# A gated recurrence with a SoLU layer behind it: weight conversions in pairs, the second group's keys turned by VectorE, loads and products of ones rearranged

## The chip, the cores and the metric

The kernel runs on one core of a Trainium2 chip. The metric is the device time of one execution in microseconds (us). It is measured in several runs; the median counts. A profile is one further execution, recorded by the hardware profiler. Names of engines: PE or TensorE (matmuls), DVE or VectorE, ACT or ScalarE, POOL or GpSimd, SP or SyncE (it only issues transfers here).

## The reference

Two blocks, one behind the other. The first is a gated linear recurrence over 768 steps, for 4 batches and 8 heads of 48 channels. The second takes its result as 3072 tokens of 384 values, multiplies by `w_in` to 1024 values, weighs each by its softmax, normalises, scales by `g_ln` and multiplies by `w_out`.

```python
for t in range(S):
    state = alpha[:, :, t, :, None] * state + np.einsum('bhd,bhe->bhde', k[:, :, t], v[:, :, t])
    y[:, :, t] = np.einsum('bhd,bhde->bhe', q[:, :, t], state)
...
x = attn_out.transpose(0, 2, 1, 3).reshape(B * S, H * D)
h = x @ w_in
e = np.exp(h - np.max(h, axis=-1, keepdims=True))
solu = h * e / (np.sum(e, axis=-1, keepdims=True) + 1e-09)
mu, var = np.mean(solu, -1, keepdims=True), np.var(solu, -1, keepdims=True)
out = ((solu - mu) / np.sqrt(var + 1e-06) * g_ln) @ w_out
```

q, k, v and alpha are float32. `w_in` (384 x 1024), `w_out` (1024 x 384) and `g_ln` are of random numbers; the two matrices come as float64 and are made into float32 on the core.

## The kernel before

**Tiling.** The 768 steps are cut into 6 groups of 128. In each group the recurrence becomes matmuls: running products of alpha along time (`scan_back`, `scan_on`, line 204) scale queries and keys, `scores` multiplies them (L278), `masked` keeps the causal half (L289), `read_values` multiplies by the values (L333), and `read_state` adds what the state of the earlier groups gives (L333 too). `keys_back` turns the scaled keys for `next_state` (L371), which brings the state to the end of the group. A group's result x has 4 batches x 128 tokens. For it, 8 slices f of 128 of the 1024 values are made: `up_mm` (three matmuls of 128x512, L394), Exp on ACT (L408), the product h times e on VectorE (L409) and its square on ACT (L412). `down` multiplies a chunk of 128 tokens by `w_out` (L513), in two halves of four f. The sums over the 1024 values come from matmuls with ones (`array_sums` L439, `token_sums` L462).

**The order is written by hand.** Each engine runs its instructions in the order in which the program gives them, and a wait holds everything behind it on that engine. The transfers named below are all issued by SP, in program order too. The body of `fast_path` from L674 to L850 is group 0 and the way into group 1; behind L933 a plan of names runs for the rest. The change touches only the first part.

**Turning.** q, k and alpha come with time along the partitions and must lie with channels along them. Group 0 does this by TensorE (`turned`, L164: a matmul with the identity, 96 of them for one tensor), group 1's k and q too (L780, L793, L805); group 1's alpha and all of the later groups go through VectorE (`firsts` L179 and `lasts` L182, called by `alpha_T` and `keys_T`). `load_first` and `load` bring the two layouts that these need; `ends_of` is ACT's copy of the last 16 channels for `turned`. `apart` (L245) parts the last channels of two heads on ACT.

**Conversion of the weights.** `w_in` and `w_out` come in 8 pieces, 0 to 3 of `w_in` (two f each), 4 to 7 of `w_out` (two f each). `fetch(i, slot, n)` loads n pieces into slots of `room` (six of 1536 words). `bit(i, k)` is step k of 5 of piece i on VectorE: two steps make the upper word (L622, L626), one its exponent (L630), one adds the lower word scaled by it (L634), and the last the sum into place (L636). Each takes 768 elements a partition. Piece i works in the two `lots` of its parity. `in_range` checks the range on ACT (L604, L607). `scaled` multiplies `w_out` by `g_ln` on ACT (L643). `u_of` puts h times e into the slots of `room` that are free by then. In the loop L753 to L778 steps of the conversions stand behind each f, by the list at L758; before it, piece 0 runs at L739 and piece 1 at L744.

**Behind the loop** come the second half of the sums, `down` of the first chunks, `mean` (L657, L664: what the mean of the normalisation takes from the output, from all of `w_out`), and group 1's decay, keys and queries. Scaled queries leave by `move_lasts` (8 transfers, L232) and `move_firsts` (4, L237) into `q64`, and `decay` (L261, on POOL) needs the last of them; `read_state` needs both.

**warm** (L452) multiplies ones by ones while TensorE has nothing else, 14 times at the start and 4 times before the queries.

Of the kernel before, what the change touches and what calls it, by code (L numbers as in the profile page):

```python
# [9 lines left out]
FP = mybir.dt.float32  # L10
U8 = mybir.dt.uint8
U32 = mybir.dt.uint32
# [4 lines left out]
P = 128  # L17
# [15 lines left out]
def fast_path(ctx, tc, q, k, v, alpha, moe_w_in, moe_w_out, moe_g_ln, out):  # L33
# [414 lines left out]

    def warm(n, ps=ps_o, tag="o"):
        t = ps.tile([P, 512], FP, tag=tag, name="warm")  # L450
        for i in range(n):
            nc.tensor.matmul(t[:, 0:P], lhsT=ones, rhs=ones, start=True, stop=True)  # L452

    def token_sums(g):

# [117 lines left out]
    def fetch(i, slot, n=1):  # L573

        kind, f = pieces[i]
        w = n * F // (2 if kind else KC)
        raw = room[:, 1536 * slot : 1536 * (slot + n)].bitcast(U32).rearrange("p (c f w) -> p c f w", f=w, w=2)
        if kind:
            parts = [(slice(0, P), c, moe_w_out[(f + c) * P : (f + c + 1) * P, :]) for c in range(2)]
        else:  # L580
            parts = [(slice(0, P), c, moe_w_in[c * P : (c + 1) * P, f * P : f * P + w]) for c in range(KC)]
        for rows, c, src in parts:
            if float64:
                nc.sync.dma_start(out=raw[rows, c].rearrange("p f w -> p (f w)"), in_=src.bitcast(U32))
            else:
                dst = w_out[rows, f + c, 0:DM] if kind else w_in[rows, c, f * P : f * P + w]
                nc.sync.dma_start(out=dst, in_=src)
        for m in range(n):
            raws[i + m] = raw[:, :, w // n * m : w // n * (m + 1)]

    far = const.tile([P, len(pieces), 2], FP, name="far")
    made = {}
# [16 lines left out]
    def bits(i, steps=range(5)):  # L609
        for k in steps if float64 else ():  # L610
            bit(i, k)

    def bit(i, k):
        lo, hi = raws[i][:, :, :, 0], raws[i][:, :, :, 1]
        if k == 0:
            made[i] = [
                lots[2 * (i % 2) + x].rearrange("p (c f) -> p c f", c=hi.shape[1]) for x in range(2)
            ]
        top, low = made[i]
        bits_top = top.bitcast(U32)  # L620
        if k == 0:
            nc.vector.tensor_scalar(  # L622
                out=bits_top, in0=hi, scalar1=3, scalar2=0x3FFFFFF8, op0=ALU.logical_shift_left, op1=ALU.bitwise_and
            )
        elif k == 1:
            nc.vector.scalar_tensor_tensor(  # L626
                out=bits_top, in0=hi, scalar=0xC0000000, in1=bits_top, op0=ALU.bitwise_and, op1=ALU.bitwise_or
            )
        elif k == 2:
            nc.vector.tensor_scalar(  # L630
                out=low.bitcast(U32), in0=bits_top, scalar1=0xFF800000, scalar2=None, op0=ALU.bitwise_and
            )
        elif k == 3:
            nc.vector.scalar_tensor_tensor(out=low, in0=lo, scalar=2.0**-52, in1=low, op0=ALU.mult, op1=ALU.mult)  # L634
        else:
            nc.vector.tensor_tensor(out=place(i), in0=low, in1=top, op=ALU.add)  # L636

    def scaled(i):

# [10 lines left out]
    def mean(half):  # L650


        m = ps_h.tile([P, 512], FP, tag="h", name="sums")[:, 0:DM]
        if half == 0:
            for f in range(FC):
                r = quarter(f % 4)
                nc.tensor.matmul(  # L657
                    m[r], lhsT=ones[:, 0:32], rhs=w_out[:, f, 0:DM], start=f < 4, stop=f >= FC - 4,
                    tile_position=(0, r.start), skip_group_check=True,
                )  # L660
            made["m"] = work.tile([P, DM], FP, name="o_mean")
# [29 lines left out]
    nc.gpsimd.memset(kg, 0.0)  # L691
    load_v(0)
    fetch(0, 3)
    fetch(1, 4)
    fetch(2, 1, 2)
    nc.vector.memset(ones, 1.0)
    nc.vector.memset(small_ones, 1.0 / 32)
    nc.vector.memset(mhalf, -0.5)
    nc.vector.memset(w_out[:, :, DM : DM + 1], 1.0)

    def three(name, where):
        return [pool.tile([P, NP, P], FP, tag=tag, name=f"{name}{i}") for i, (pool, tag) in enumerate(where)]
# [20 lines left out]
    for i in (0, 2, 1):  # L723
        if i == 1:
            scan_on(0, i)
        part = slice(NP * i, NP * i + NP)
        nc.vector.tensor_tensor(
            out=qe[:, :, 0:P] if i == 2 else qv[:, part, 0:P], in0=t[i], in1=aT[:, part, 1:SW], op=ALU.mult
        )
        if i == 2:  # L730
            apart()
    scores(0, 0)
    t = [x.tile([P, NP, P], FP, tag=n, name="a_" + n) for x, n in ((ps_h, "h"), (ps_o, "o")) for _ in range(2)]
    scores(0, 1, t)
    read_begin()
    for half in range(2):
        masked(half, range(B - 1))
        masked_apart(half, B - 1)
    bits(0)  # L739
    read_values(0)  # L740
    gains()
    keys_back(0)
    in_range(0)
    bits(1)  # L744

    steps = [(i, step) for i in range(2, 8) for step in range(5)]
    checks = {0: [(2, 0)], 1: [(2, 1)], 2: [(3, 0)], 3: [(3, 1)], 4: [(1, 0), (1, 1)], 5: [(4, 0), (4, 1)]}

    def check(f):
        for i, part in checks.get(f, ()):  # L750
            in_range(i, (part,))

    for f in range(FC):  # L753
        up_mm(0, f)
        if f == 4:
            array_sums(0, 0)
        up_act(0, f, lambda: check(f))
        for _ in range((4, 2, 3, 3, 3, 3, 3, 9)[f]):  # L758
            step = steps.pop(0)
            if float64:  # L760
                bit(*step)
        if f == 0:
            next_state(0)
            fetch(4, 3)
            load_first(k, kn, 1)
            load_first(q, qn, 1)
            load(alpha, an, 1)
        elif f == 2:
            ends_k = ends_of(kn, "e")
        elif f == 3:  # L770
# [36 lines left out]
    hold(1)  # L807
    keys_back(1, three("tp", [(ps_a, "a2"), (ps_a, "a3"), (ps_h, "h")]))
    scan_on(1, 2)
    nc.vector.tensor_tensor(out=qe[:, :, 0:P], in0=tq[2], in1=aT[:, H:NB, 1:SW], op=ALU.mult)  # L810
# [656 lines left out]
```

## Time and profile before

| | |
|---|---|
| median of 3 runs | 366.96 us (366.78 to 367.19) |
| the profiled execution | 368.38 us |
| its span, first to last instruction | 366.6 us |
| granted TensorE clock | 0.998 |
| VectorE busy, 20 to 30 / 60 to 70 / 90 to 100 us | 9.58 / 9.79 / 9.83 of 10 |
| ACT busy, 40 to 50 / 50 to 60 us | 8.26 / 7.09 of 10 |
| first matmul with `w_in` | 29.64 us |
| last step of the conversions | ends at 63.92 us |
| `read_state` of group 1 | 88.63 us |
| first matmul of group 1 with `w_in` | 97.58 us |

A line of the timeline gives start and length in us, engine, line of the program and operation, the tile that is written and those that are read, the shape, and how many alike stand together (x). In brackets stands how long the engine had been idle before and what it waited for; "issue" means nothing that the profile shows. PE is the matmul, PEld the load of its weights. A float32 matmul makes two records, so x24 is twelve matmuls. The ends of matmuls are modelled, so the distance of two starts says more than a length. A DMA window lists what each queue moved in that stretch: packets, MB and the time of its packets as a share of 16 engines.

### The profile page before, as it was taken

How to read it: one execution, taken by the hardware profiler on the slowest of the kernel's cores; microseconds unless marked ns; L12 is line 12 of the kernel's file. 1: busy time of each engine (PE TensorE's matmuls, PEld its weight loads, DVE VectorE, ACT ScalarE, POOL GpSimd, SP SyncE). 2: the span in 40 equal slices, each digit the busy share in tenths (PEclk: the TensorE clock that was granted, in tenths of full speed). 3: DMA queues.
4: the chain of work that ended last, by engine and by line, in shares of the span. 5: the costliest groups of instructions: out<-in, count | busy, mean ns of one | idle time of the engine just before them, and what ended most of it. 6: DMA issues, size and time to landing. Idle time of an engine off the chain costs nothing. (4 is left out here: it accounts for less than half of the span.)

```text
span 366.6 us, 10041 instructions
## 1 busy us (share of the span) xinstructions
PE 358.0 (98%) x4341; PEld 216.0 (59%) x4341; DVE 243.9 (67%) x375; ACT 146.5 (40%) x262; POOL 130.3 (36%) x127
## 2 busy tenths in 40 slices
PE   8989999999999999999999999999999999999994
PEld 8866345666655566556475556575556565555552
DVE  0999989979997796936665946766946404445420
ACT  3637887372736261252531253531242222222110
POOL 7020000003368663764232763332773121233300
PEclk9999999999999999999999999999999999999999
DMA  9994997326196509354044454004042000000011
GB/s 178 186 333 139 194 302 156 88 59 146 68 222 133 131 4 192 90 123 123 5 108 92 103 115 113 21 25 88 21 96 66 0 25 1 23 21 22 23 46 51
DMA packets 72871, 36.06 MB, mean 98 GB/s; under 512 B 48232, under 2 KB 70000, under 8 KB 72816
## 3 DMA queue, kind: packets, MB, share of 16 engines
q1 hardware_dynamic: 71792, 34.39, 39.6%
q10 hardware_dynamic: 1024, 0.92, 0.8%
q8 instruction: 36, 0.59, 0.7%
q14 instruction: 19, 0.16, 0.1%
HBM read 25.30 MB, written 4.72 MB: 82 GB/s over the span
## 5 line engine op out<-in xcount | busy, mean ns | idle before, releaser
L513 PE MATMUL o<-w_out,room 128*128 128x385 f32 x384 | 133.8, 491 | 0.0
L394 PE MATMUL h<-x,w_in 128*128 128x512 f32 x288 | 131.6, 597 | 0.0
L513 PEld LDWEIGHTS o<-w_out,room 128*128 128x128 f32 x384 | 71.1, 189 | 55.2 <-issue 13.4
L394 PEld LDWEIGHTS h<-x,w_in 128*128 128x128 f32 x288 | 53.2, 189 | 58.0 <-issue 49.0
L409 DVE TENSOR_TENSOR room<-h,e 128x512 f32<-128x512 f32 x40 | 27.6, 690 | 72.7 <-ACT e L408 72.7
L408 ACT ACTIVATE e<-h 128x512 f32<-128x512 f32 x40 | 23.9, 598 | 98.9 <-PE h L394 98.9
L427 POOL TENSOR_TENSOR p<-p,e 128x512 f32<-128x512 f32 x30 | 43.1, 1437 | 20.3 <-ACT e L408 20.2
L412 ACT ACTIVATE u<-room 128x512 f32<-128x512 f32 x40 | 25.2, 630 | 37.0 <-DVE room L409 37.0
L552 POOL TENSOR_TENSOR r<-sums,mhalf 128x1 f32<-128x1 f32 x20 | 14.8, 740 | 67.9 <-DVE sums L543 67.7
L289 DVE TENSOR_TENSOR sT<-a,mask 128x512 f32<-128x512 f32 x43 | 26.7, 682 | 8.7 <-PE a L278 8.7
L204 DVE TENSOR_TENSOR_SCAN hT<-aT,unit 128x516 f32<-128x516 f32 x18 | 24.3, 1396 | 7.9 <-ACT aT L709 7.8
L204 DVE TENSOR_TENSOR_SCAN aT<-aT,seed 128x516 f32<-128x516 f32 x18 | 25.4, 1441 | 0.2
L225 POOL TENSOR_TENSOR kT<-kT,hT 128x1024 f32<-128x1024 f32 (+1 forms) x8 | 13.3, 1687 | 33.6 <-DVE kT L179 33.6
L278 PEld LDWEIGHTS a<-qv,kT 32*128 32x128 f32 x704 | 21.1, 186 | 6.8 <-issue 2.4
L427 DVE TENSOR_TENSOR p<-p,u 128x512 f32<-128x512 f32 x30 | 21.7, 723 | 5.1 <-ACT u L412 5.1
L333 PE MATMUL y<-sT,vn 128*32 128x128 f32 x768 | 23.3, 274 | 1.6 <-issue 1.4
L278 PE MATMUL a<-qv,kT 32*128 32x128 f32 x704 | 23.7, 279 | 0.2 <-ACT qv L245 0.2
L212 POOL COPY fend<-hT 128x12 f32<-128x12 f32 x6 | 3.0, 507 | 56.4 <-DVE hT L204 56.4
L333 PEld LDWEIGHTS y<-sT,vn 128*32 128x32 f32 x768 | 20.9, 110 | 3.5 <-issue 2.7
L196 ACT ACTIVATE sq<-an,mone 128x1536 uint8<-128x1536 f32 x12 | 18.9, 1572 | 0.2
L554 ACT ACTIVATE o_sb<-o,r 128x384 f32<-128x384 f32 x16 | 9.3, 580 | 18.5 <-POOL r L552 18.5
L261 POOL TENSOR_TENSOR state<-state,lot 128x384 f32<-128x384 f32 x10 | 8.8, 902 | 15.6 <-DMA lot<-qv 15.6
(150 smaller groups left out, 376.7 us busy)
## 6 DMA issues: line engine op xcount, KB each, us to landing
vn<-in_v_dram SPq DMA_DIRECT2D x24, 192.0 KB, 4.7
an<-in_alpha_dram SPq DMA_DIRECT2D x20, 192.0 KB, 4.0
out_dram<-o_sb SPq DMA_DIRECT2D x20, 192.0 KB, 1.9
room<-in_moe_w_out_dram SPq DMA_DIRECT2D x8, 384.0 KB, 5.6
kn<-in_k_dram SPq DMA_DIRECT2D x16, 192.0 KB, 4.8
qn<-in_q_dram SPq DMA_DIRECT2D x16, 192.0 KB, 3.8
lot<-qe SPq DMA_DIRECT2D x40, 64.5 KB, 2.1
lot<-qv SPq DMA_DIRECT2D x20, 129.0 KB, 2.4
```

The costliest lines, as they stand in the source:

```text
L196: nc.scalar.activation(out=sq, in_=x, func=AF.Relu, scale=sign, bias=mone, accum_out=over[:, g, i : i + 1])
L204: nc.vector.tensor_tensor_scan(out=o, data0=a, data1=s, initial=1.0, op0=ALU.mult, op1=ALU.add)
L278: nc.tensor.matmul(a[b][:, i], lhsT=kT[quarter(b), kb], rhs=qv[quarter(b), qb, 0:P], start=not last and not i, stop=bool(last), tile_posit ...
L289: nc.vector.tensor_tensor(out=sT[:, b, half * NP : half * NP + NP], in0=a[b], in1=mask[:, None, :].to_broadcast([P, NP, P]), op=ALU.mult,)
L333: nc.tensor.matmul(y_bank(b)[quarter(r), a], lhsT=lhsT, rhs=rhs, start=(b, r) not in begun, stop=stop, tile_position=(row, 32 * r), skip_g ...
L394: nc.tensor.matmul(h, lhsT=w_in[:, a, f * P : (f + 1) * P], rhs=d["x"][:, a].rearrange("p b t -> p (b t)"), start=(a == 0), stop=(a == KC ...
L408: nc.scalar.activation(out=e, in_=h, func=AF.Exp)
L409: nc.vector.tensor_tensor(out=u, in0=h, in1=e, op=ALU.mult)
L412: nc.scalar.activation(out=u2, in_=u, func=AF.Square)
L427: eng.tensor_tensor(out=p, in0=d[0][i] if f == 1 else p, in1=d[f][i], op=ALU.add)
L513: nc.tensor.matmul(d["o"][:, 0 : DM + 1], lhsT=u_of(g, f)[:, b * P : b * P + P], rhs=w_out[:, f], start=(f == 0), stop=(f == FC - 1), skip ...
L552: nc.gpsimd.tensor_tensor(out=r, in0=s[:, 3:4], in1=mhalf, op=ALU.pow)
```

## The change

- `warm` makes products up to 512 wide, four of the old ones in one.
- `fetch` lays several pieces one behind the other in `room`, each contiguous; before, the rows of two pieces lay side by side. So slot 1 and slot 2 each hold one piece.
- The loads of pieces 1, 2 and 3 are issued behind `apart` of group 0: ACT writes one column of slot 4 there, and the load into that slot waits for it.
- Piece 0 is converted in halves of 128 columns, in an order in which the first half ends two steps ahead of the second.
- Pieces 1 to 7 are converted with the steps of piece i + 1 between those of piece i; how many stand behind each f changes. Piece 7's last step goes to POOL.
- Checks and scalings on ACT move: piece 4 is checked at f 4, piece 1 at f 5, `scaled(4)` and `scaled(5)` come at f 6.
- `fetch` of piece 5 comes at f 1, alpha's load at f 3 behind piece 6. Group 1's k is loaded by `load` instead of `load_first`.
- `turned` of group 1's keys is left out; `keys_T(1)` stands behind the conversions.
- The order behind the loop: `down`, sums, two scalings, `down`, keys, sums by token, alpha, then all of q in one piece; the products of keys one step later than their scans; `scan_on(1, 0)` before the first product of queries. `mean` takes a bank of `ps_a`.

```diff
     def warm(n, ps=ps_o, tag="o"):
         t = ps.tile([P, 512], FP, tag=tag, name="warm")
-        for i in range(n):
-            nc.tensor.matmul(t[:, 0:P], lhsT=ones, rhs=ones, start=True, stop=True)
+        for c in range(0, n, 4):
+            w = P * min(4, n - c)
+            x = ones[:, None, :].to_broadcast([P, w // P, P])
+            nc.tensor.matmul(t[:, 0:w], lhsT=ones, rhs=x, start=True, stop=True)
...
-        raw = room[:, 1536 * slot : 1536 * (slot + n)].bitcast(U32).rearrange("p (c f w) -> p c f w", f=w, w=2)
+        raw = room[:, 1536 * slot : 1536 * (slot + n)].bitcast(U32)
+        raw = raw.rearrange("p (m c f w) -> p c m f w", m=n, f=w // n, w=2)
...
-            raws[i + m] = raw[:, :, w // n * m : w // n * (m + 1)]
+            raws[i + m] = raw[:, :, m]
...
-    def bit(i, k):
+    def bit(i, k, part=None):
...
+        if part is not None:
+            lo, hi, top, low, dst = (x[:, :, P * part : P * part + P] for x in (lo, hi, top, low, dst))
...
-            nc.vector.tensor_tensor(out=place(i), in0=low, in1=top, op=ALU.add)
+            (nc.gpsimd if i == 7 else nc.vector).tensor_tensor(out=dst, in0=low, in1=top, op=ALU.add)
...
-        m = ps_h.tile([P, 512], FP, tag="h", name="sums")[:, 0:DM]
+        m = ps_a.tile([P, 512], FP, tag="a3", name="sums")[:, 0:DM]
...
     fetch(0, 3)
-    fetch(1, 4)
-    fetch(2, 1, 2)
...
+    def fetch_more():
+        nc.scalar.copy(out=slots[4][:, 0:1], in_=parity[:, 0:1])
+        fetch(1, 4)
+        fetch(2, 1, 2)
...
             apart()
+            fetch_more()
...
-    bits(0)
+    bits((0, k, part) for k, part in ((0, 0), (0, 1), (1, 0), (1, 1), (2, 0), (2, 1), (3, 0), (4, 0), (3, 1), (4, 1)))
...
-    bits(1)
-
-    steps = [(i, step) for i in range(2, 8) for step in range(5)]
-    checks = {0: [(2, 0)], 1: [(2, 1)], 2: [(3, 0)], 3: [(3, 1)], 4: [(1, 0), (1, 1)], 5: [(4, 0), (4, 1)]}
+    steps = [(1, 0), (1, 1)]
+    for i in range(1, 8):
+        steps += [(i, 2), (i + 1, 0), (i, 3), (i + 1, 1), (i, 4)]
+    steps = [x for x in steps if x[0] < 8]
+    for a, b in (((2, 1), (1, 4)), ((6, 1), (5, 4))):
+        i, j = steps.index(a), steps.index(b)
+        steps[i], steps[j] = b, a
...
+    convert(5)
+    checks = {0: [(2, 0)], 1: [(2, 1)], 2: [(3, 0)], 3: [(3, 1)], 4: [(4, 0), (4, 1)], 5: [(1, 0), (1, 1)]}
 
     def check(f):
         for i, part in checks.get(f, ()):
             in_range(i, (part,))
+        if f == FC - 2:
+            scaled(4)
...
-        for _ in range((4, 2, 3, 3, 3, 3, 3, 9)[f]):
-            step = steps.pop(0)
-            if float64:
-                bit(*step)
+        convert((5, 2, 3, 3, 4, 3, 2, 8)[f])
         if f == 0:
             next_state(0)
             fetch(4, 3)
-            load_first(k, kn, 1)
+            load(k, kn, 1)
             load_first(q, qn, 1)
+        elif f == 1:
+            fetch(5, 1)
+        elif f == 3:
+            fetch(6, 2)
             load(alpha, an, 1)
-        elif f == 2:
-            ends_k = ends_of(kn, "e")
-        elif f == 3:
-            fetch(5, 1)
-            fetch(6, 2)
             ends_q = ends_of(qn, "u2")
         elif f == 5:
             fetch(7, 3)
             load_v(1)
         elif f == 6:
-            scaled(4)
-    tk = three("tp_k", [(ps_a, "a2"), (ps_a, "a3"), (ps_h, "h")])
-    turned(kn, ends_k, tk)
+            scaled(5)
+    down(0, 0)
+    array_sums(0, 1)
+    scaled(6)
+    scaled(7)
+    down(1, 0)
+    keys_T(1)
     load(k, kn, 2)
-    array_sums(0, 1)
-    scaled(5)
-    down(0, 0)
-    scaled(6)
+    token_sums(0)
     alpha_over(1)
-    token_sums(0)
     alpha_T(1)
     load(alpha, an, 2)
-    down(1, 0)
-    scaled(7)
-    tq = three("tp_q", [(ps_a, "a0"), (ps_a, "a1")])
-    turned(qn, ends_q, tq, range(H))
-    for i in range(3):
-        scan_back(1, i)
-        part = slice(NP * i, NP * i + NP)
-        nc.vector.tensor_tensor(out=kT[:, part], in0=tk[i], in1=hk[:, part], op=ALU.mult)
+    tq = three("tp_q", [(ps_a, "a0"), (ps_h, "h"), (ps_a, "a2")])
+    turned(qn, ends_q, tq)
+    for i in (0, 1, None, 2):
+        if i is not None:
+            scan_back(1, i)
+        for j in {1: (0,), None: (1,), 2: (2,)}.get(i, ()):
+            part = slice(NP * j, NP * j + NP)
+            nc.vector.tensor_tensor(out=kT[:, part], in0=kT[:, part], in1=hk[:, part], op=ALU.mult)
     inverses(1)
     mean(0)
...
-    tq += three("tp_q2", [(ps_h, "h")])
-    turned(qn, ends_q, tq, range(H, NB))
     down(1, 1)
     hold(1)
-    keys_back(1, three("tp", [(ps_a, "a2"), (ps_a, "a3"), (ps_h, "h")]))
+    keys_back(1, three("tp", [(ps_a, "a1"), (ps_a, "a3"), (ps_h, "h")]))
     scan_on(1, 2)
+    scan_on(1, 0)
...
     for i in range(2):
-        scan_on(1, i)
+        if i:
+            scan_on(1, i)
```

More of the change, by code (lines that the diff above doesn't have):

```diff
@@ L583, in fetch @@
             if float64:
-                nc.sync.dma_start(out=raw[rows, c].rearrange("p f w -> p (f w)"), in_=src.bitcast(U32))
+                nc.sync.dma_start(
+                    out=raw[rows, c].rearrange("p m f w -> p m (f w)"),
+                    in_=src.bitcast(U32).rearrange("p (m x) -> p m x", m=n),
+                )
             else:
@@ L607, in in_range, with bits @@
             nc.scalar.activation(out=sq, in_=sq, func=AF.Exp, scale=-(2.0**24), accum_out=far[:, i, 1:2])
-    def bits(i, steps=range(5)):
-        for k in steps if float64 else ():
-            bit(i, k)
-    def bit(i, k):
+    def bits(steps):
+        for x in steps if float64 else ():
+            bit(*x)
+    def bit(i, k, part=None):
         lo, hi = raws[i][:, :, :, 0], raws[i][:, :, :, 1]
-        if k == 0:
+        if k == 0 and not part:
             made[i] = [
@@ L618, in bit @@
             ]
+        dst = place(i)
         top, low = made[i]
+        if part is not None:
+            lo, hi, top, low, dst = (x[:, :, P * part : P * part + P] for x in (lo, hi, top, low, dst))
         bits_top = top.bitcast(U32)
@@ L743, in fast_path, with convert @@
     in_range(0)
-    bits(1)
-    steps = [(i, step) for i in range(2, 8) for step in range(5)]
-    checks = {0: [(2, 0)], 1: [(2, 1)], 2: [(3, 0)], 3: [(3, 1)], 4: [(1, 0), (1, 1)], 5: [(4, 0), (4, 1)]}
+    steps = [(1, 0), (1, 1)]
[5 more added lines that the diff above has]
+        steps[i], steps[j] = b, a
+    def convert(n):
+        bits(steps[:n])
+        del steps[:n]
+    convert(5)
+    checks = {0: [(2, 0)], 1: [(2, 1)], 2: [(3, 0)], 3: [(3, 1)], 4: [(4, 0), (4, 1)], 5: [(1, 0), (1, 1)]}
     def check(f):
```

## The prediction

> **What bounds the kernel now.** I read, in this order: busy time by engine; TensorE's timeline of the first 125 us (does it ever stop?); the timelines of VectorE and of the DMA queue in the same stretch; the DMA windows around the one stop.
>
> ```profile
> PE 358.0 (98%) x4341; PEld 216.0 (59%) x4341; DVE 243.9 (67%) x375; ACT 146.5 (40%) x262; POOL 130.3 (36%) x127
> 23.09 0.64 PE L333 MATMUL y<-sT,vn 128*32 128x128 f32 x14 [0.20 <-DVE sT L289]
> 25.15 3.04 PE L333 MATMUL y<-sT,vn 128*32 128x128 f32 x102 [1.41 <-issue]
> 29.64 2.74 PE L394 MATMUL h<-x,w_in 128*128 128x512 f32 x6
> ...
> 54.08 1.96 PE L164 MATMUL tp_k<-ident,kn 128*32 128x128 f32 x64
> 55.85 1.06 PE L164 MATMUL tp_k<-ident,e 128*32 128x128 f32 x32
> 56.73 1.90 PE L439 MATMUL quarters<-sT,ones 128*32 128x512 f32 x16
> ...
> 88.63 1.19 PE L333 MATMUL y<-lot,state 64*32 64x128 f32 x64
> ```
>
> After 25.15 no line has an idle note until the tail, so TensorE is the bound: every microsecond that it starts later, or that is taken from its list, counts, if its inputs keep up. The 1.41 us have no releaser. Around them the DMA window 22.0 to 22.7 shows one packet of the instruction queue among full data queues; the windows from 15 to 22 have none.
>
> ```profile
> q1 hardware_dynamic: 142, 0.26, 103.2%
> q8 instruction: 1, 0.02, 8.7%
> ```
>
> Next to TensorE stands VectorE, which has hardly a gap from 8.9 to 79 us. Its starts show two prices:
>
> ```profile
> 38.79 0.94 DVE L622 TENSOR_SCALAR lot<-room 128x768 uint32<-128x768 uint32 x1
> 57.33 0.56 DVE L630 TENSOR_SCALAR lot<-lot 128x768 uint32<-128x768 uint32 x1
> 57.92 0.96 DVE L634 SCALAR_TENSOR_TENSOR lot<-room,lot 128x768 f32<-128x768 uint32 x1
> 58.92 0.96 DVE L636 TENSOR_TENSOR w_out<-lot 128x768 f32<-128x768 f32 x1
> 59.80 0.55 DVE L622 TENSOR_SCALAR lot<-room 128x768 uint32<-128x768 uint32 x1
> ```
>
> L634 is followed by its reader L636 after 1.00 us; L636 by an unrelated instruction after 0.88. So a neighbour that reads the result costs 0.12 more. And L622 takes 0.94 for pieces 2 and 3, 0.56 for the others.
>
> Last, the chain that ends at read_state (88.63):
>
> ```profile
> 74.50 0.69 DVE L810 TENSOR_TENSOR qe<-tp_q,aT 128x512 f32<-128x512 f32 x1
> 75.26 5.26 SPq L232 DMA_DIRECT2D lot<-qe  x8
> 80.62 3.16 SPq L237 DMA_DIRECT2D lot<-qv  x4
> 85.18 1.65 POOL L261 TENSOR_TENSOR state<-state,lot 128x384 f32<-128x384 f32 x2 [12.38 <-DMA lot<-qv]
> ```
>
> qe ends at 75.19, the state is decayed at 86.83, and read_state could begin about 0.15 later: qe's end plus 11.8 = 87.0. TensorE came at 88.63, so 1.6 us of slack.
>
> **The Trainium skill.** "Runtime: NRT & Kernel Launch", Instruction fetch mechanics: instructions come in 16 KiB blocks of 256 over a DMA queue of the sequencer's own. The trace agrees (36 packets, 0.59 MB, 16 KB each); the page calls the cost mostly hidden, here it is 1.41 us. "VectorE: DVE Perf Modes", Mode 2×_2P: two read ports serve one tensor if the outermost dimension is even, or odd and equal in source and destination. Agrees: pieces 2 and 3 read 3 separate runs of 256 (odd) into one run of 768, 0.94 us; the single runs take 0.56. [...]
>
> **Part by part.**
>
> *Wide ones.* 14 and 4 products become 4 and 1; a product is two weight loads and two matmuls, so 13 fewer products are 52 fewer instructions. The columns stay, so the first warm keeps its 6.03 us (estimate): a shorter one gains nothing (alpha lands at 7.0, where ACT's copy waits 4.84 us for it), a longer one costs its excess. The second stands before a wait for qn.
>
> *w_in behind the parting.* One ACT copy of a column (about 0.2, in a gap of 0.93 before L297), then 6 of the 9 issues move from about 18 to 19.9. Nothing later on SP wants to go before 31. The packet at 22.68 came behind what was issued before its request, I take it: three or four w_in loads. Now only v and piece 0 are ahead, and the block boundary lies 52 instructions later. Bounds: stall 0 to 1.4; I take 0.2. Pieces 2 and 3 then land near 28, wanted from 30.4.
>
> *First half of piece 0.* Without the stop, batch 3's mask (POOL, done 24.42) is not late, and four batches of 16 products at 0.058 end at 26.5. Then tp_g 0.15 and keys_back 1.37 (28.27 to 29.64): h begins at 28.0, with the 0.2 at 28.2, so 1.44 earlier. Its weights: piece 0 in halves. 768 elements at 0.56/0.96 give 384 at about 0.36/0.56 (half of the slope); eight of ten steps from 24.15, with the 0.2 that L622 lost there to POOL (0.74 against 0.56), end at 27.6: in time. All ten take 4.4, against 4.25 before. If halves fell to the slower mode, 0.8 more, and h at 28.4.
>
> *Conversions side by side.* Pieces 1 to 7 had 28 dependent neighbours, 6 of them parted by L409; now 4 remain: 18 x 0.12 = 2.2. L622 of pieces 2 and 3: 2 x 0.38 = 0.76. Piece 7's addition goes to POOL: 0.88. The last conversion ended at 63.84: 63.84 - 3.84 = 60.0. VectorE's waits in this stretch were 1.37 (0.28, 0.16, 0.20, 0.36, 0.37). Walking the new order with h groups of 2.62 from 28.2, I find 0.1 at f 5, 0.6 at f 6 and 0.85 at f 7, because ACT has 3.2 to 3.4 us in each of f 4 to 6 against TensorE's 2.62 (four checks, then two scalings of 1.05, the second before the last Exp). So 1.5 against 1.4: no change, 60.0 stands.
>
> *Loads.* On SP k goes with the plain load (4 issues, 3.3 us), then q (4.4), piece 5, piece 6, then alpha (3.4), wanted at 61 only. Piece 5 is issued near 40 instead of 44 and wanted at 44.8; landing took 5.6: covered, barely. The moved in_range(1) frees slot 4 for u 6 in time.
>
> *Keys by VectorE.* TensorE loses 96 products, all that runs from 54.08 to 56.73: 2.65 us. VectorE gains two transposes, by the starts of the next group's (95.87, 97.76, 98.69) 2.82. The copy of k's ends leaves ACT (0.61). No matmul waits for them before keys_back. The products with hk then read kT from SBUF instead of PSUM: 0.69 as now, since L427's additions of that size from SBUF take 0.66 to 0.69. mean's bank moves to a3, free since the first group's a3 was read.
>
> *Order of the tail.* VectorE from 60.0: keys 2.82, cols 0.37, alpha 2.91, scans and products 1.15 + 1.15 + 0.61 + 0.61 + 1.27 + 0.61, reciprocal 0.26, two scans 2.30, qe 0.69: 74.75, against 75.19. qv's first part follows at 75.4, so scores are free. POOL's addition of 768 (1.19 for 512, 2.19 for 1024, so 1.7) ends at 61.8, scaled(7) at 63; mean(0) is due at 63.2. Bounds 1.4 to 2.2; at 2.2 TensorE waits 0.4. ACT then has alpha_over, 3.3 us, ahead of o_mean: mean(1) waits about 0.85.
>
> *Sum.* TensorE's own arrival at read_state: 88.63 - 1.44 - 2.65 + 0.85 = 85.4. The query chain: 74.75 + 11.8 = 86.6, and that is later. So 2.0 us are gained of 4.1, and the lists behind are unchanged and shift as a whole (VectorE is 2 to 3 us ahead there). Span 366.6 - 2.0 = 364.6. The profiled execution took 368.38, 1.8 around its span and 1.4 over the median 366.96; on the median, 365.0.
>
> **Rivals.**
> - *TensorE stays the bound.* ACT's waits turn out smaller and qe comes by 73.5. Then 85.4 holds: 3.2 gained, 363.7. For it: TensorE never stops now. Against: the lengthened ACT order.
> - *The fetch stays late.* Stall 1.4: h at 29.4, Exps about 1.0 later, qe at 75.75, read_state 87.5: 1.1 gained, 365.9. For it: the same 0.8 MB of piece 0 lies in front.
> - *Piece 5 is late.* Its first step stands before L409 of f 5 in VectorE's order; 2 us of waiting there take the whole gain: 367.0.
> - *Slower: VectorE's list.* Pairing saves nothing, because the 0.12 belongs to the instruction kinds and not to the dependency. Then 60.0 becomes 62.2 and the tail 0.57 longer: qe at 77.5, read_state at 89.3, 0.7 late: 367.7. It decides from qe's end at 88.63 - 11.8 = 76.8. Against it: wherever the next instruction is unrelated, it starts 0.08 before L636 or L409 ends.
>
> **How the numbers follow.** Forecast 0.45, TensorE-bound 0.17, fetch 0.15, piece 5 0.11, VectorE 0.12. What the measurement tells from no change is 0.2%, 0.73 us. Faster: 0.45 + 0.17 + 0.13 of the fetch case = 0.75; same: 0.09 of piece 5 and 0.02 = 0.11; slower: 0.12 + 0.02 = 0.14. The range 363.3 to 366.9 holds the forecast with its unknowns, most of the TensorE-bound case, the fetch case and half of piece 5.
>
> **What would show it.** The pause at 25.15 shrunk, h near 28.2, L622 at 0.56 for all whole pieces, conversions ended near 60, qe near 74.8, read_state near 86.6 with POOL's decay just in front of it. Wrong if qe ends after 76.8, if a VectorE line before L409 of f 5 waits for a load, or if the first h starts after 29.4.

## The result, and the profile after

The changed kernel takes 368.33 us (median of 22 runs, 366.52 to 371.06), the kernel before 366.94 (22 runs, 366.62 to 367.61). The ratio is 1.0041, interval 1.0031 to 1.0052: 1.4 us slower, where 2 us less was forecast. The changed kernel's times also spread over 4.5 us, those of the kernel before over 1.0. Runs over 1.5% above the fastest of the same kernel are left out of every median and ratio below (two of the first experiment's eleven, one of six in the first with 3 products of ones more).

In the three slowest runs of the changed kernel (370.21 to 371.06) the granted clock of TensorE was 0.989 to 0.992; in its other 19 runs it was 0.996 or more. What lowers it is shown below, with the twelve instructions.

The profiled execution has a span of 367.5 us. First the timeline of TensorE, the lines with which parts begin or which have an idle note:

```profile
27.71 2.74 PE L394 MATMUL h<-x,w_in 128*128 128x512 f32 x6
32.17 1.23 PE L371 MATMUL kv<-vn,kg 128*32 128x48 f32 x97 [1.25 <-issue]
...
68.45 0.91 PE L673 MATMUL sums<-o_mean,ones 128*128 128x384 f32 x2 [0.86 <-ACT o_mean L671]
...
87.36 0.55 PE L333 MATMUL y<-lot,state 64*32 64x128 f32 x16 [0.52 <-POOL state L261]
...
93.18 0.42 PE L333 MATMUL y<-lot,state 64*32 64x128 f32 x8 [1.48 <-issue]
...
142.73 1.13 PE L515 MATMUL o<-w_out,room 128*128 128x385 f32 x3 [0.83 <-issue]
```

The stop of 1.41 us in y is gone and h begins 1.93 us sooner. But three new stops without a releaser stand in kv, in read_state and in the products with `w_out`. Group 1's first h comes at 98.57, before at 97.58. Then VectorE's timeline:

```profile
32.82 0.56 DVE L631 TENSOR_SCALAR lot<-room 128x768 uint32<-128x768 uint32 x1 [2.16 <-DMA room<-in_moe_w_in_dram]
...
57.05 0.55 DVE L631 TENSOR_SCALAR lot<-room 128x768 uint32<-128x768 uint32 x1
57.53 0.96 DVE L643 SCALAR_TENSOR_TENSOR lot<-room,lot 128x768 f32<-128x768 uint32 x1
58.40 0.96 DVE L635 SCALAR_TENSOR_TENSOR lot<-room,lot 128x768 uint32<-128x768 uint32 x1
59.27 0.96 DVE L645 TENSOR_TENSOR w_out<-lot 128x768 f32<-128x768 f32 x1
...
75.89 0.66 DVE L831 TENSOR_TENSOR qe<-tp_q,aT 128x512 f32<-128x512 f32 x1
```

The pairs work: from L643 to L635 and on to L645 it is 0.87 us from start to start, where a dependent neighbour took 1.00 before. But the first step of piece 2 waits 2.16 us for its load. SP had issued all nine loads of `w_in` by 23.5. Here is the data queue in four DMA windows: 24 to 26 before; 24 to 26 and 27 to 29 after; 24 to 26 in a later profile of the changed kernel, the third, in which nothing waits for `w_in`:

```profile
q1 hardware_dynamic: 231, 0.81, 102.2%
```

```profile
q1 hardware_dynamic: 153, 0.30, 84.8%
q1 hardware_dynamic: 411, 0.80, 103.4%
```

```profile
q1 hardware_dynamic: 270, 0.52, 90.1%
```

The layout with one piece behind the other cuts a row that two pieces shared: pieces 2 and 3 now come in packets of 2048 bytes, where they came in packets of 4096 before. It is tempting to blame that. But from 27 to 29 the short packets carry 0.80 MB in 2 us, as much as the long ones before (0.81). From 24 to 26 packets of the same length carried 0.30 MB in one profile and 0.52 in another. So this stretch was slow for another reason, which differs from one execution to the next and stays open.

### The profile page after: what moved, and what is told of

Its sections match the earlier page's. It is cut to its first block, busy times and chain, and to the rows that moved or that the text cites. A ratio compares the mean times of both kernels' runs of the same rounds, so it can differ in the third digit from the quotient of the medians.

```text
span 367.5 us, 9811 instructions
## 1 busy us (share of the span) xinstructions
PE 354.6 (96%) x4219; PEld 209.0 (57%) x4219; DVE 242.8 (66%) x381; ACT 146.7 (40%) x262; POOL 131.8 (36%) x128
## 5 line engine op out<-in xcount | busy, mean ns | idle before, releaser
L427 POOL TENSOR_TENSOR p<-p,e 128x512 f32<-128x512 f32 x30 | 42.2, 1407 | 20.3 <-ACT e L408 20.2
L204 DVE TENSOR_TENSOR_SCAN hT<-aT,unit 128x516 f32<-128x516 f32 x18 | 23.5, 1355 | 7.5 <-ACT aT L721 7.5
L645 POOL TENSOR_TENSOR w_out<-lot 128x768 f32<-128x768 f32 x1 | 1.8, 1845 | 37.6 <-DVE lot L643 37.6
```

Source lines behind the costliest of these rows:

```text
L204: nc.vector.tensor_tensor_scan(out=o, data0=a, data1=s, initial=1.0, op0=ALU.mult, op1=ALU.add)
L427: eng.tensor_tensor(out=p, in0=d[0][i] if f == 1 else p, in1=d[f][i], op=ALU.add)
```

## What the stops are

I counted TensorE's instructions (weight loads, matmuls and its waits on semaphores) in the order of the trace. The stop in y before stands ahead of number 961, those after ahead of 1217, 2497 and 4289: all are 193 more than a multiple of 256. In the twenty profiles of this study, from 10 us on, 26 starts come more than 0.75 us after the one before them without a releaser and with the engine idle in between; all 26 stand at 193 modulo 256. From the start of the last packet of the instruction queue to the next instruction it is 2.27 to 3.00 us, in every one of them.

So a stop is a block of 256 instructions that came too late. Where the queues are free and TensorE does not wait, its packet starts about 1 us after TensorE has crossed the boundary before it (crossed at 93.18, packet at 94.22). Behind the gated loads it took 6 us (23.81, 29.76: the stop in kv); in the third profile, where these loads had drained sooner, 4 us (23.89, 27.77), and kv has no stop. In read_state the boundary was crossed at 85.72, and this is SP's timeline there, then two DMA windows of the changed kernel, 88 to 90.2 and 90 to 91:

```profile
85.66 1.92 SPq L134 DMA_DIRECT2D qn<-in_q_dram  x4
```

```profile
q1 hardware_dynamic: 608, 0.43, 98.5%
```

```profile
q1 hardware_dynamic: 49, 0.03, 15.4%
q8 instruction: 1, 0.02, 7.2%
```

The packet starts at 90.67, when the 0.8 MB of qn's load have drained: 5 us after the crossing. The block that was running lasted 5.7 us, and 5 + 2.5 is more. The load is not all of the 5 us, though. In an experiment below it is issued 17 us sooner. There the boundary was crossed at 84.31 and these are the windows 85.5 to 87.5 and 87.5 to 88.5:

```profile
q1 hardware_dynamic: 1, 0.00, 0.0%
```

```profile
q8 instruction: 1, 0.02, 5.9%
```

The data queue is empty, and still the packet starts at 88.05 only, 3.7 us after the crossing (3.5 in the second profile of that kernel). TensorE waits for POOL's decay in between, until 86.43. So the load adds 1.1 to 1.5 us here, which is about what the stop measures (1.48; 1.23 in the third profile). What exactly asks for a packet is not settled.

Two pages of the Trainium skill bear on this. "Runtime: NRT & Kernel Launch", Instruction fetch mechanics, has the sequencer fetch the next 16 KiB page while it executes the current one; that agrees. It calls the cost mostly hidden: here it is hidden at most boundaries, and 0.2 to 3.1 us where not. "DMA: Bandwidth & Descriptors", Queues, rings and completion order, has each engine take turns between its queues, with turns of typically 9 to 17 descriptors and at most 64. In the window above a packet took 0.057 us (608 packets, 98.5% of 16 engines for 2.2 us). If such a packet is one descriptor, a turn is at most 3.7 us by estimate; the 1.1 to 1.5 us that the load adds would fit into one turn. No run here shows the turns themselves.

The boundaries do not move with the work. The pages of the two profiles count them:

```profile
PE 358.0 (98%) x4341; PEld 216.0 (59%) x4341; DVE 243.9 (67%) x375; ACT 146.5 (40%) x262; POOL 130.3 (36%) x127
```

```profile
PE 354.6 (96%) x4219; PEld 209.0 (57%) x4219; DVE 242.8 (66%) x381; ACT 146.7 (40%) x262; POOL 131.8 (36%) x128
```

122 matmuls and 122 weight loads fewer are 244 instructions, 256 less 12. So from group 1 on every boundary falls 12 instructions earlier in the work than before.

## The experiments

In the first four expectations L is the theory of the late loads, F that of the instruction blocks.

**Loads early.** The changed kernel without the gate:

```diff
     fetch(0, 3)
+    fetch(1, 4)
+    fetch(2, 1, 2)
     nc.vector.memset(ones, 1.0)
...
-            fetch_more()
```

> The changed kernel with the loads of pieces 1 to 3 issued where the kernel before issued them (no gate behind the parting). Theory L (late loads: VectorE's 2.16 us wait for piece 2 eats the early start, everything behind slips): that wait falls from 2.16 to under 0.3, the conversions end near 60 instead of 61.7, qe near 75, and the median is 366.0 to 367.0, some 1.5 to 2 under the changed kernel's 368.3. Theory F (instruction blocks: TensorE's stops of 1.25 in kv and 1.48 in read_state come from where the block boundaries fall): the wait goes, but a stop of 1 to 1.5 comes back in y near 24, the one in read_state stays, and the median is 367.8 to 368.6.

369.09 us (nine runs; 369.26 with all eleven), ratio 1.0048 (1.0035 to 1.0062). The wait for piece 2 is 0.69, and a stop of 0.36 is back in y. That the edit shortened the wait is not shown: with the gate kept it was 2.16 and none in two profiles of the changed kernel and 0.69 with only qn's load moved; with the loads early again, further below, it was 1.67. But the time is not better, and the stop in read_state is there too:

```profile
91.76 0.42 PE L333 MATMUL y<-lot,state 64*32 64x128 f32 x8 [1.50 <-issue]
```

**Wide rows.** The gate stays, pieces 2 and 3 lie side by side again:

```diff
-        raw = raw.rearrange("p (m c f w) -> p c m f w", m=n, f=w // n, w=2)
+        raw = raw.rearrange("p (c f w) -> p c f w", f=w, w=2)
...
-            raws[i + m] = raw[:, :, m]
+            raws[i + m] = raw[:, :, w // n * m : w // n * (m + 1)]
```

> The changed kernel, gate kept, but pieces 2 and 3 lie side by side in room as before, so their packets are 4096 bytes instead of 2048 (384 x 162 ns instead of 768 x 106 ns, 1.2 us less of all 16 engines). Theory L: VectorE's wait for piece 2 falls from 2.16 to about 1, L631 takes 0.94 again for two pieces (0.76 more), median 367.5 to 368.2. Theory F: nothing moves at the boundaries, median 368.0 to 368.6. If the packet size were the whole cause, the wait would be under 0.3.

375.22 us, ratio 1.0221 (1.0188 to 1.0253). The wait for piece 2 is 1.24, inside what the changed kernel itself shows (2.16 and none), so the price of the short packets is not told from this. And VectorE now waits here, and TensorE 3.33 us behind it:

```profile
47.00 0.96 DVE L640 SCALAR_TENSOR_TENSOR lot<-room,lot 128x768 f32<-128x768 uint32 x1 [4.48 <-DMA room<-in_moe_w_out_dram]
```

That is an effect of the edit on something else. Side by side, pieces 2 and 3 share slots 1 and 2, and the program puts the load of piece 5 into slot 1 at f 1. The fourth step of piece 3 comes at f 2, still reads slot 1, and so waits for that load and reads piece 5's lower words there. The layout of one piece behind the other is what lets piece 5 be loaded at f 1. So the 2.2% say nothing of the packets.

**Narrow products of ones.** The changed kernel with `warm` as before, 52 instructions more:

```diff
-        for c in range(0, n, 4):
-            w = P * min(4, n - c)
-            x = ones[:, None, :].to_broadcast([P, w // P, P])
-            nc.tensor.matmul(t[:, 0:w], lhsT=ones, rhs=x, start=True, stop=True)
+        for i in range(n):
+            nc.tensor.matmul(t[:, 0:P], lhsT=ones, rhs=ones, start=True, stop=True)
```

> The changed kernel with the narrow products of ones: 52 more TensorE instructions ahead of all others, same columns. Theory F: every block boundary falls 52 instructions earlier; the stop of 1.48 in read_state (the boundary fell between its dense products) goes or shrinks below 0.5, the one in kv may move into y; the median differs from 368.3 by 0.7 or more, either way. Theory L: nothing that it rests on changes, median 368.0 to 368.7, VectorE's wait for piece 2 again near 2.

369.8 us, ratio 1.0081 (1.0055 to 1.0106). Stops in kv, read_state and near 142 are gone; one of 1.75 has come in h, at 36.88, while the loads of f 0 run.

**The gate alone.** The kernel before, with only the loads of pieces 1 to 3 behind `apart`:

```diff
-    fetch(1, 4)
-    fetch(2, 1, 2)
...
             apart()
+            nc.scalar.copy(out=slots[4][:, 0:1], in_=parity[:, 0:1])
+            fetch(1, 4)
+            fetch(2, 1, 2)
```

> The kernel before with only the gate: loads of pieces 1 to 3 behind the parting. Theory L: its order wants piece 2 only at 33.7, so VectorE waits under 0.5; the loads by themselves cost nothing here and the median is 366.4 to 367.3. Theory F: the stop of 1.41 in y shrinks or moves to kv, at most 1.4 gained: 365.6 to 367.0, unless a later boundary now meets a busy queue.

368.41 us, ratio 1.0024 (1.0010 to 1.0038): slower. The stop in y goes as forecast (h at 28.84) and comes back in h:

```profile
36.67 8.31 PE L394 MATMUL h<-x,w_in 128*128 128x512 f32 x19 [1.19 <-issue]
```

Four runs moved stops about without removing their cost. In the next four, theory Q is F with one thing added: a block is asked for when TensorE crosses the boundary before it.

**qn's load sooner.** The changed kernel:

```diff
     turned(qn, ends_q, tq)
+    load(q, qn, 2)
...
     move_firsts()
-    load(q, qn, 2)
```

> The changed kernel with one load at another place in SP's order: group 2's qn (4 issues, 192 KB each) stands behind alpha's load near 70 us instead of behind move_firsts at 85.66. Theory Q (a block of 256 TensorE instructions is asked for when the boundary before it is crossed; at 85.72 this request meets qn's load, issued at 85.66, and the block lands at 90.67 instead of about 1 us after the crossing): the block lands near 86.7, the stop of 1.5 us in read_state near 93 is gone, the first h of group 1 comes near 97.1 instead of 98.57, the wait of 1.25 in kv and the one of 0.83 near 142 stay or shift as a whole; median about 1.2 to 1.5 us under the changed kernel's 368.3, so 366.9. Theory L (the late pieces 2 and 3 alone are what is lost): nothing changes, 368.3.

In the profile read_state has no stop, group 1's h comes at 95.88 and the span is 365.4. The packet did not come near 86.7, as Q had it, but at 88.05, just in time. Yet the median is 368.5, ratio 1.0036 (1.0018 to 1.0055): no gain that can be told from the changed kernel's. Two of the idle notes that are left:

```profile
86.43 0.55 PE L333 MATMUL y<-lot,state 64*32 64x128 f32 x16 [0.99 <-POOL state L261]
...
140.37 1.13 PE L515 MATMUL o<-w_out,room 128*128 128x385 f32 x3 [1.03 <-issue]
```

**52 instructions late.** 13 products of 32x16 in the wait for `mean`:

```diff
-        m = ps_a.tile([P, 512], FP, tag="a3", name="sums")[:, 0:DM]
+        m = ps_a.tile([P, 512], FP, tag="a3", name="sums")
+        for i in range(13 * half):
+            nc.tensor.matmul(
+                m[0:32, DM : DM + 16], lhsT=ones[:, 0:32], rhs=ones[:, 0:16], start=True, stop=True, skip_group_check=True
+            )
+        m = m[:, 0:DM]
```

> The changed kernel with 13 products of 32x16 (52 TensorE instructions) in TensorE's wait for the second half of mean, near 67.6 us; they go to unused columns and are read by nobody. Theory Q: the boundaries behind fall 52 instructions earlier in the work, the request crosses before qn's load is issued, and both later stops (1.5 near 93, 0.8 near 142) go, while the kv stop of 1.25 at 32 stays: first h of group 1 near 97.2, median 366.0 to 366.8. If only the amount of work counts: the same as the changed kernel or up to 0.5 slower, 368.3 to 368.8.

368.87 us, ratio 1.0045 (1.0033 to 1.0057): the expectation failed. Both later stops are gone, but moved boundaries are moved in all five later groups. Set against the run before it instruction by instruction, this one gains 1.2 us near 140 and loses 0.8 near 186 and 0.6 near 294.

**Both with the loads early.** Two combinations with the first run's edit.

> The changed kernel with the loads of w_in's pieces 1 to 3 at their old place (as in the first run of this study, 369.26 with stops of 1.50 at 91.76 and 1.22 at 141.78) and qn's load behind alpha's. Theory Q: the stop in read_state goes, that at 142 stays, read_state near 86; median about 1.5 under 369.26, so 367.7, or lower where the spread of that run came from the same stop. Theory L: as that run.

371.57 us, ratio 1.0132 (1.0105 to 1.0159); a stop of 1.72 in y.

> The changed kernel with the loads at their old place and the 13 small products in the wait for mean. Theory Q: both later stops go, the small one near 24.7 (0.36) stays, read_state near 86.2, first h of group 1 near 96, span about 364.3; median 365.5 to 366.6, under both kernels. If the stops only move to other loads: 367 to 369.

370.14 us, ratio 1.0074 (1.0055 to 1.0093); a stop of 1.48 in y. Both expectations failed: in these two profiles the stop in y is longer than it was in the kernel before.

**The same kernels again.** Four more profiles, of the kernel before, of the changed one (twice) and of the one with qn's load sooner.

> The kernel before, unchanged, profiled a second time. Theory S (stops at the boundaries of instruction blocks come and go from one execution to the next, and the profiled executions are samples of them): the stop of 1.41 at 25.15 may be missing or of another length, and the span differs from 366.6 by what the stops differ. Theory P (the stops belong to the kernel and recur): 1.41 at 25.15 again, span 366.6 within 0.2.

> The changed kernel, unchanged, profiled a second time. Theory S: another set of stops than 1.25 in kv, 1.48 in read_state and 0.83 near 142; the span is 364.4 plus the stops that are not covered by another wait. Theory P: the same three, span 367.5.

> The changed kernel profiled a third time. The same two theories as for the second profile: S another set of stops and a span between 364.4 and 368, P the same three and 367.5.

> The changed kernel with qn's load behind alpha's, profiled a second time. Its times lay at 367.2 to 367.6 in four executions and at 368.5 to 370.4 in five. Theory S: no stop in read_state in this profile either, but the one in kv or y may be there, and the span is then 366 to 367. Theory P: only the one near 140, span 365.4.

Theory S (stops come and go from one execution to the next) holds for all stops but one. The kernel before, second profile (span 365.8, execution 367.56):

```profile
24.12 3.04 PE L333 MATMUL y<-sT,vn 128*32 128x128 f32 x102 [0.36 <-issue]
28.64 2.81 PE L394 MATMUL h<-x,w_in 128*128 128x512 f32 x6
...
35.66 8.31 PE L394 MATMUL h<-x,w_in 128*128 128x512 f32 x19 [0.36 <-issue]
...
96.95 2.74 PE L394 MATMUL h<-x,w_in 128*128 128x512 f32 x6
```

1.41 has become 0.36. The changed kernel, third profile (span 366.8, execution 368.62):

```profile
27.80 2.74 PE L394 MATMUL h<-x,w_in 128*128 128x512 f32 x6
...
86.00 0.55 PE L333 MATMUL y<-lot,state 64*32 64x128 f32 x16 [1.00 <-POOL state L261]
...
91.61 0.42 PE L333 MATMUL y<-lot,state 64*32 64x128 f32 x8 [1.23 <-issue]
97.09 2.74 PE L394 MATMUL h<-x,w_in 128*128 128x512 f32 x6
...
141.62 1.13 PE L515 MATMUL o<-w_out,room 128*128 128x385 f32 x3 [1.22 <-issue]
```

No stop in kv here, and VectorE does not wait for piece 2 at all. In the second profile y had one of 2.29, and read_state no stop but a wait of 2.37 ahead of it; behind both the granted clock was about half for more than 3 us (0.50 from 28 to 31, 0.52 from 92.5 to 96), and the span is 372.0. The fourth, with qn's load sooner, has a span of 365.8 and no stop in read_state. Only the stop near 141 is in every profile of this order of TensorE's work, whichever loads are early: 0.83, 1.34 and 1.22 in the changed kernel, 1.03 and 0.69 with qn's load sooner, 1.22 and 0.54 with the early loads.

**Twelve instructions.** If the place of a boundary decides, 12 instructions can be worth microseconds. All four runs have qn's load sooner; `SC` puts `scan_on(1, 0)` back behind qe.

```diff
     warm(4, ps_a, "a1")
+    few = ps_a.tile([P, 512], FP, tag="a1", name="few")
+    for i in range(3):
+        nc.tensor.matmul(few[0:32, 0:16], lhsT=ones[:, 0:32], rhs=ones[:, 0:16], start=True, stop=True)
```

> The changed kernel with qn's load behind alpha's, and 3 products of 32x16 (12 TensorE instructions) behind the second warm, whose result nobody reads. All boundaries of blocks behind fall 12 instructions earlier in the work, where the kernel before has them. Theory Q: the stop of 0.7 to 1.3 us near 141 that all six profiles of this order have goes, the block that is crossed at 19.6 is asked for 0.2 us before the gated loads and never lands late, so no stop in y; the one in kv may stay. Span 364.4 to 365.0, median 366.2 to 367.2 against 368.5 for the same kernel without the 3 products. If the position of the boundaries does not matter: 368.5.

> As the run before it, and scan_on(1, 0) back behind qe on VectorE, so that qe ends 1.0 us sooner (near 73.7) and read_state stops waiting for POOL's decay (0.99 and 1.24 in the two profiles without it). Theory Q: read_state near 85.5, span 363.6 to 364.3, median 0.5 to 1.0 under the run before it: 365.5 to 366.5, faster than both kernels. If the waits of read_state only turn into a stop for instructions: no gain over the run before it.

> The changed kernel with qn's load behind alpha's and scan_on(1, 0) behind qe, without the 3 products. Theory Q: qe near 73.7, read_state near 85.5, but the stop near 141 stays: about 1.0 us over the run with the 3 products; median 367 to 367.8. If the boundaries do not matter: the same as that run.

Without `SC`, 373.94 us (five runs; 1.0175, 1.0136 to 1.0213) against 368.5 (1.0036) for the same without the 3 products. With `SC`, 371.37 (1.0116, 1.0082 to 1.0149) against 367.55 (22 runs, 1.0017, 1.0004 to 1.0029). Place decides, but my sign was wrong: the kernel before has its boundaries 12 later in the work, not 12 earlier, so the products put them 24 off. TensorE's timeline with the 3 products and `SC`:

```profile
135.86 1.57 PE L371 MATMUL kv<-vn,kg 128*32 128x48 f32 x128
137.24 0.63 PE L464 MATMUL rows<-p,ones 128*32 128x64 f32 x31
140.92 0.22 PE L464 MATMUL rows<-p,ones 128*32 128x64 f32 x1 [3.05 <-issue]
```

and without them:

```profile
138.03 0.64 PE L464 MATMUL rows<-p,ones 128*32 128x64 f32 x32
138.60 1.89 PE L515 MATMUL o<-w_out,room 128*128 128x385 f32 x5
140.80 1.13 PE L515 MATMUL o<-w_out,room 128*128 128x385 f32 x3 [0.31 <-issue]
```

256 instructions of kv are 1.57 us of work, so this block runs out before any fetch can come. What lies between it and the boundary is the cover: no more than 31 records of 0.02 us in the first case, five records of 0.4 us in the second.

The stop is not the whole cost. TensorE's busy time, its matmuls and the granted clock in two stretches behind it, with the 3 products and without:

```profile
141.00:144.00 3.00, 3.00 (x7) 0.70 0.76 147
144.00:148.00 4.00, 4.00 (x9) 0.80 0.45 104
```

```profile
141.00:144.00 3.00, 3.00 (x9) 1.00 1.00 173
144.00:148.00 4.00, 4.00 (x13) 1.00 0.89 207
```

The clock is the third number from the right. At 0.70 for 3 us and 0.80 for 4 us, 1.7 us of work are lost. With the stop's 2.74 more (3.05 against 0.31) that is 4.4 us, and the spans differ by 4.3 (370.0 and 365.7). In the twenty profiles, from 10 to 360 us, the clock falls seven times. Each time it falls to 0.50, for 3.4 us (once 6.8), during a pause of TensorE of 2.29 to 3.33 us or within 1.4 us of its end; it never falls after a pause of 1.75 us or less. Pauses between 1.75 and 2.29 us did not occur.

> As the second of these runs, and piece 1 converted alone, so that piece 2 is wanted two steps (1.8 us) later. Theory L: the wait of VectorE for piece 2 (2.16, 1.81, 1.06, 0.69 and none in the profiles of this order) is gone, at a price of 3 dependent neighbours (0.36 us); where it was over 0.4 that is gained, so median 0.3 to 1.0 under the second run and a narrower spread. Theory Q alone: 0.3 us slower than the second run, since VectorE's waits for ACT take up what the load gives.

```diff
-    steps = [(1, 0), (1, 1)]
-    for i in range(1, 8):
+    steps = [(1, k) for k in range(5)] + [(2, 0), (2, 1)]
+    for i in range(2, 8):
...
-    for a, b in (((2, 1), (1, 4)), ((6, 1), (5, 4))):
+    for a, b in (((6, 1), (5, 4)),):
```

371.14 us (1.0113, 1.0077 to 1.0150), against 371.37 with piece 1 paired: VectorE's wait for piece 2 is gone from the profile, and the time is the same within the intervals.

**Twelve fewer, and 244 more.** With `SC`; the first has `warm(8)` for `warm(14)` and no second `warm`, the second has 61 products more, mostly of 32x16.

> The third run of the last group (changed kernel, qn's load behind alpha's, scan_on(1, 0) behind qe: 367.55) with 3 products of ones fewer: warm makes 2 at the start instead of 4, and none before the queries. 12 TensorE instructions fewer put all boundaries behind 12 instructions later in the work, which is where the kernel before has them. Theory Q: no stop near 141 (it was 0.3 to 1.3 there, and 3.1 with 12 more), median 0.5 to 1.0 lower: 366.6 to 367.0, level with the kernel before or just faster. Against it: the earlier boundary of 19.6 comes 0.2 us later and so behind the gated loads, and a stop of 2.3 in y as in one profile is likelier; or TensorE is slow after the shorter warm, at up to 1 us. Then 368 to 369.

> The same third run with 61 products of ones more, most of them 32x16, in the places of warm and in the wait for k: 244 TensorE instructions, 256 less 12, so the boundaries lie as in the run with 3 products fewer while TensorE stays busy. Theory Q: the same as that run within 0.5, no stop near 141, 366.6 to 367.2. If it is the number of instructions and not their place modulo 256 that counts: far off that run, 369 and more.

12 fewer: 366.35 us (22 runs, 364.83 to 368.34), ratio 0.9983 (0.9970 to 0.9996): faster than the changed kernel, and than the kernel before by a margin (0.17%) that its interval just clears. 244 more: 367.17 (1.0000, 0.9989 to 1.0010). Neither profile has a stop near 141. With 12 fewer:

```profile
6.79 3.35 PE L164 MATMUL tp_a<-ident,an 128*32 128x128 f32 x58 [1.35 <-DMA an<-in_alpha_dram]
...
24.00 3.47 PE L333 MATMUL y<-sT,vn 128*32 128x128 f32 x116 [0.20 <-DVE sT L289]
...
138.12 0.64 PE L464 MATMUL rows<-p,ones 128*32 128x64 f32 x32
138.69 2.86 PE L515 MATMUL o<-w_out,room 128*128 128x385 f32 x8
```

The eight products with `w_out` now stand before the boundary and cover the fetch. The gain stands although the shorter `warm` costs time: alpha is turned more slowly and y begins at 24.00 instead of 23.39. Shifts of −12 and of +244 agree in place and differ by 256 instructions; 12 more is 4 to 5 us worse than either. So the cost follows where the boundaries lie, not how many instructions there are; the 0.8 us between these two runs is not explained.

## Why the prediction was wrong

One row for each profile; "rest" is the span less the start of group 1's h.

| us | before | before, 2nd | after | after, 3rd | 12 fewer |
|---|---|---|---|---|---|
| first h | 29.64 | 28.64 | 27.71 | 27.80 | 28.92 |
| qe begins | 74.50 | 74.00 | 75.89 | 74.05 | 74.90 |
| group 1's h | 97.58 | 96.95 | 98.57 | 97.09 | 97.19 |
| rest | 269.0 | 268.9 | 268.9 | 269.7 | 268.2 |
| stops | 1.41 | 0.36, 0.36 | 1.25, 1.48, 0.83 | 1.23, 1.22 | none |

**The sum, first failure.** "The profiled execution took 368.38, 1.8 around its span and 1.4 over the median 366.96; on the median, 365.0." The 1.8 is right: it is 1.8 to 1.9 in all these profiles. But I subtracted the 1.4 as a constant. It has the size of the stop of 1.41 in y, which this execution had and the second has not (0.36 there). At 1.8, the median belongs to a span of 365.2, which is 366.6 less the stop. So about 1 us of the "1.44 earlier" was not in the median and could not be gained there. That is worked out from two profiles; a timed run leaves no trace in which to see its stops. Without this step the forecast would have been 364.6 + 1.8 = 366.4.

**The sum, second failure.** "The lists behind are unchanged and shift as a whole." The lists do, the boundaries do not. A stop of 0.3 to 1.3 us near 141 is new in every profile of this order, and the runs with 12 instructions more, 12 fewer and 244 more show that this place counts in the timed runs as well. I had priced blocks at one spot only ("the block boundary lies 52 instructions later") and put all later ones at nothing. Also new in two of three profiles is the stop in read_state: TensorE now arrives just as qn's load is issued. In the third profile the two measure 2.45 us. From 366.4 they lead to 368.85; this execution took 368.62, and the median is 368.33.

**The loads.** "Pieces 2 and 3 then land near 28, wanted from 30.4." In the first profile VectorE waited 2.16 us for piece 2, up to 32.8; the prediction had named such a wait ahead of f 5 as a sign of being wrong. In the third profile no piece of `w_in` waits, so it is another cost that comes and goes; removing it (piece 1 alone) moved no median.

**What was right.** Without the stop h begins at 27.7 to 27.8 (28.2 forecast). L631 takes 0.55 to 0.58 for all whole pieces. VectorE's waits for ACT are 0.15, 0.35 and 0.80, at f 4, 6 and 7 (0.1, 0.6 and 0.85 at f 5, 6 and 7). mean(1) waits 0.86 (0.85). POOL's sum takes 1.84 (1.7). In the third profile, where no load of `w_in` is late, VectorE is done with the conversions at 59.76 (60.0), qe ends at 74.71 (74.75) and read_state begins at 86.00 behind POOL's decay (86.6). So the named bound at read_state, the query chain, is the right one. Taking the third profile's two stops off its span leaves 366.8 − 2.45 = 364.4, against 364.6 forecast; that is worked out and not a run. But the kernel before, also without most of its stop, ends qe at 74.69: at qe there is no gain, and up to group 1's h it is 1.1 us (96.95 against 97.09 − 1.23).

**The rivals.** None of them was it. The fetch was a rival at the old place, not at new ones. VectorE's list did end late in the first profile (qe at 76.55), but through the wait for piece 2, not because pairing saves nothing. Piece 5's first step waited 0.55 us in the third profile and not at all in the first, where 2 us were named.

**Open.** How often the stops in y, kv and read_state come in timed runs is not settled: profiles are few, and qn's load sooner, which removed the one in read_state in both its profiles, did not move the median by what can be measured. Nor is it settled what made the loads of `w_in` slow from 24 to 26, and how often the clock falls in timed runs.

## To carry to other kernels

A stop without a releaser in a profile is one sample: take a second profile of the kernel before, or compare its span with the median less the usual margin, before a gain is counted on its going. When an edit changes the number of instructions of the busiest engine, find where its blocks of 256 now end: a short block (small matmuls, 1.6 us for 256) with loads in flight and little long work behind it cost 0.3 to 3.1 us here, and a few instructions more or fewer move it. Look last at the granted clock behind a long pause, and do not take packets of another length for the cause of a late load before a window with the same packets has been compared.

## What was not expected of the hardware

- TensorE goes on 2.27 to 3.00 us after the start of the instruction packet (26 stops); the packet itself took 0.9 to 1.5 us.
- In read_state the packet starts 4.8 to 5.0 us after the crossing with qn's 0.8 MB in the queues (three profiles) and 3.5 to 3.7 with empty queues (two).
- 3 products of 32x16 made the kernel about 4 to 5 us slower (367.55 to 371.37, 368.5 to 373.94), 3 products fewer 1.2 us faster (367.55 to 366.35).
- A pause of TensorE of 2.29 us or more goes with a clock of 0.50 for 3.4 us, 1.7 us of work on top of the pause (seven times, once for 6.8 us); pauses of 1.75 us or less left it at 1.00.
